# Attention and a feed-forward layer in one kernel: a rebuilt prologue (full-partition weight loads, two load queues, first token tile in two column parts, first output tile K-outer, one batch's loads moved later)

## The chip, the cores and the metric

One core of one Trainium2 chip. The metric is the device time of one execution in microseconds (us), median of several executions; lower is better. In the profiles PE is the matmul engine and PEld its weight loads, DVE is VectorE, ACT ScalarE, POOL GpSimd; SP, the sync engine, only issues transfers (DMA). PSUM is the memory that matmuls write to.

## The reference, cut to what matters

```python
# q, k, v: (8, 8, 576, 64) f32; w_in: (512, 2048); w_out: (2048, 512)
k_p = k.reshape(B, H, 72, 8, D).mean(axis=3)      # 8 keys are averaged into one
v_p = v.reshape(B, H, 72, 8, D).mean(axis=3)
attn = softmax(q @ k_p.T / sqrt(D)) @ v_p         # per batch and head
x = attn.transpose(0, 2, 1, 3).reshape(4608, 512)
h = x @ w_in
out = (h * sigmoid(h)) @ w_out                    # (4608, 512) f32
```

## The kernel before: the parts that matter

The 4608 tokens are cut into 9 tiles of 512; a batch is 576 tokens, so tile t needs the attention of batches up to t. Attention of batch 0 is a prologue. From then on tile t's matmuls carry batch t+1's attention as "fillers", each attached to a step number (0 to 63) of the tile's up-projection (`up`) or down-projection (`down`). Nothing reorders them: an engine's stream is the order of this program.

```python
def load_q(b):                       # f32, two loads of 64 partitions each
    q_raw = big.tile([128, H // 2, QI * D], FP32, tag="q_raw", name="q_raw")   # 2 buffers
    for g in range(2):
        nc.sync.dma_start(out=q_raw[64 * g : 64 * (g + 1), :, :], in_=...)
def load_kv(b):                      # batches 2 to 7: 72 partitions, 1 buffer each
    for name, src in (("k", k), ("v", v)):
        raw = big.tile([SP, H, POOL * D], FP32, tag=f"{name}_raw", bufs=1, name="raw")
        nc.sync.dma_start(out=raw, in_=...)
# (cut) load_kv_flat: batches 0 and 1, k on partitions 0-63 and v on 64-127

def up(t, fillers):                  # (cut) 16 groups of 4 matmuls hp_ps, then Silu -> h_T
def down(t, h_T, fillers):
    for m in range(4):               # one block of 128 tokens after the other
        for g in range(KG):          # 16 matmuls o_ps, K inner
            ...
        nc.vector.tensor_copy(out=o_sb, in_=o_ps)
        # (cut) two stores of 64 partitions on nc.sync

load_q(0); load_kv_flat(0, 3); load_q(1)
# (cut) w_in: 16 loads of 32 partitions on gpsimd; w_out: 4 loads
load_kv_flat(1, 1)
# (cut) attention of batch 0; softmax's division is Ln and Exp on ACT
for t in range(NT):
    a = t + 1
    if a + 1 < B:
        f_up.append((0, lambda: load_q(a + 1)))      # batch t+2, a whole tile ahead
    f_up.append((0, lambda: cast_q(a)))              # GpSimd, f32 -> bf16
    ...
    if a + 1 < B:
        f_up.append((51, lambda: load_kv(a + 1)))
    for n in range(4):                               # PE transposes of the cast q
        f_up.append((20 + 8 * n, lambda n=n: q_transpose(a, n // 2, n % 2)))
```

So in tile 0 the kernel issues batch 2's q, k and v, which tile 1 needs. They are called **batch 2's loads** below.

The softmax here doesn't subtract the row's maximum and nothing guards it: scores larger than these inputs give would overflow.

## Time and profile before

| | before |
|---|---|
| median | 350.74 us (3 runs, 350.31 to 351.3) |
| span of the profiled run | 350.2 us |
| PE busy | 308.6 us, 88% |
| mean granted PE clock | 0.981 |
| up of tile 0 / down of tile 0 / tile 1 / tile 2 start (first matmul in the timeline) | 37.19 / 58.51 / 86.57 / 120.48 us |

The page's rows of 40 slices (each 8.8 us; a digit is tenths):

```profile
PE   0336878499999999999999999999999999999994
PEclk9999989679999999999999999999999999999999
DMA  7999999612866296628653964496420021022022
```

PE is full from the ninth slice on. Ahead of it lie slices full of transfers, and a dip of PE in the eighth, where it waits for `w_out`. Two groups of the page, with busy us and mean ns | idle time before them and what ended it:

```profile
L319 PE MATMUL o_ps<-w_out_sb,h_T 128*128 128x512 bf16 x576 | 142.9, 385 | 6.1 <-DMA w_out_sb<-in_moe_w_out_dram 6.1
L121 PE MATMUL qT_ps<-ident,q_bf 128*128 128x128 bf16 x144 | 14.1, 233 | 12.8 <-POOL q_bf L109 12.7
```

Of the 12.7 us, 10.3 are one wait in the prologue and 2.42 one in tile 0's up; tile 1 has none.

### The profile page before, as it was taken

What the parts mean: (1) busy time and instruction counts of PE and PEld (TensorE: products, weight loads), DVE (VectorE), ACT (ScalarE), POOL (GpSimd) and SP (SyncE); (2) the same over time, 40 slices, a digit from 0 to 9 for tenths busy, and PEclk for the clock granted to TensorE, in tenths of its full rate; (3) what the DMA queues carried; (4) which work ended last, traced back from release to release, by engine and by line L of the source; (5) the groups of instructions that cost most, each with busy time, mean ns of one, the idle gap of its engine ahead of it and who ended that gap; (6) DMA issues with size and microseconds to landing.
All of it is one profiled execution on the core that took longest, in us unless ns stands there. A gap on an engine that the chain in (4) does not pass through costs nothing.

```text
span 350.2 us, 4636 instructions
## 1 busy us (share of the span) xinstructions
PE 308.6 (88%) x1858; PEld 146.0 (42%) x1858; DVE 137.3 (39%) x204; ACT 177.3 (51%) x299; POOL 50.3 (14%) x61
## 2 busy tenths in 40 slices
PE   0336878499999999999999999999999999999994
PEld 0212334144544454445444544454445444444441
DVE  0641651033653456365546553754376231020011
ACT  1026628045675566555755665566566656604600
POOL 2731232000060006000500240033000000000000
PEclk9999989679999999999999999999999999999999
DMA  7999999612866296628653964496420021022022
GB/s 170 223 249 238 238 239 216 121 32 62 176 142 153 59 204 135 154 61 194 138 137 72 204 143 110 93 198 140 96 60 0 21 63 40 0 60 63 0 55 65
DMA packets 21221, 42.24 MB, mean 121 GB/s; under 512 B 2000, under 2 KB 4048, under 8 KB 21072
## 3 DMA queue, kind: packets, MB, share of 16 engines
q1 hardware_dynamic: 17808, 37.76, 47.2%
q0 software_dynamic: 3392, 4.20, 6.8%
q8 instruction: 14, 0.23, 0.3%
q14 instruction: 7, 0.06, 0.1%
HBM read 36.70 MB, written 9.44 MB: 132 GB/s over the span
## 4 chain that ended last, share of the span: by engine, by line
PE 74%; DMA 17%; ACT 4%; POOL 1%; issue 1%; SPq 0%; DVE 0%; POOLq 0%
PE o_ps L319 33%; PE hp_ps L299 32%; DMA w_in_sb<-in_moe_w_in_dram 8%; DMA w_out_sb<-in_moe_w_out_dram 7%; PE sc_ps L235 4%; ACT L277 2%; DMA q_raw<-in_q_dram 2%; PE nu_ps L260 2%; PE den_ps L252 2%; PE qT_ps L121 2%; ACT es L242 1%; ACT h_T L306 1%; POOL q_bf L109 1%; POOL w_out_sb L361 0%; PE kT_ps L165 0%
## 5 line engine op out<-in xcount | busy, mean ns | idle before, releaser
L319 PE MATMUL o_ps<-w_out_sb,h_T 128*128 128x512 bf16 x576 | 142.9, 385 | 6.1 <-DMA w_out_sb<-in_moe_w_out_dram 6.1
L299 PE MATMUL hp_ps<-xT,w_in_sb 128*128 128x512 bf16 x576 | 134.5, 385 | 0.0
L306 ACT ACTIVATE h_T<-hp_ps 128x512 bf16<-128x512 f32 x144 | 85.8, 597 | 70.5 <-PE hp_ps L299 70.4
L319 PEld LDWEIGHTS <-h_T 128*128 128x128 bf16 x576 | 56.2, 99 | 67.4 <-issue 15.8
L299 PEld LDWEIGHTS <-w_in_sb 128*128 128x128 bf16 x576 | 55.4, 99 | 61.6 <-issue 3.9
L272 DVE TENSOR_TENSOR xT<-nu_ps,rec 128x288 bf16<-128x288 f32 x64 | 26.3, 453 | 98.8 <-ACT rec L270 87.5
L109 POOL CAST q_bf<-q_raw 128x576 bf16<-128x576 f32 x32 | 37.0, 1196 | 167.0 <-PE qT_ps L121 118.6
L242 ACT ACTIVATE es<-sc_ps 72x576 bf16<-72x576 f32 x64 | 41.4, 647 | 28.4 <-PE sc_ps L235 28.2
L326 DVE COPY o_sb<-o_ps 128x512 f32<-128x512 f32 x36 | 24.8, 690 | 62.4 <-PE o_ps L319 62.4
L145 DVE TENSOR_TENSOR raw<-raw 72x2048 f32<-72x2048 f32 (+1 forms) x24 | 44.8, 1868 | 0.4
L235 PE MATMUL sc_ps<-qT,kz 128*72 128x288 bf16 x128 | 28.5, 307 | 7.7 <-ACT es L242 7.7
L268 ACT ACTIVATE lnd<-den_ps 128x288 f32<-128x288 f32 x32 | 13.1, 410 | 31.8 <-PE den_ps L252 31.8
L127 DVE COPY qT<-qT_ps 128x640 bf16<-128x640 bf16 (+1 forms) x32 | 14.5, 458 | 35.1 <-PE qT_ps L121 35.1
L121 PE MATMUL qT_ps<-ident,q_bf 128*128 128x128 bf16 x144 | 14.1, 233 | 12.8 <-POOL q_bf L109 12.7
L235 PEld LDWEIGHTS <-kz 128*72 128x72 bf16 x128 | 15.4, 122 | 21.5 <-issue 12.3
L121 PEld LDWEIGHTS <-q_bf 128*128 128x128 bf16 x144 | 11.2, 105 | 20.0 <-POOL q_bf L109 13.6
L260 PE MATMUL nu_ps<-es,vp 72*32 72x288 bf16 x256 | 14.8, 311 | 0.5 <-ACT lnd L268 0.5
L270 ACT ACTIVATE rec<-lnd 128x288 f32<-128x288 f32 x32 | 14.2, 445 | 1.0
L219 ACT COPY vT<-kvT_ps 64x160 bf16<-64x160 bf16 (+1 forms) x8 | 2.2, 274 | 21.5 <-DVE kz L216 21.3
L280 ACT ACT_TABLE_LOAD x9 | 11.5, 1283 | 0.2
L277 ACT ACT_TABLE_LOAD x8 | 10.3, 1283 | 0.9 <-PEq L420 0.7
L351 POOL DMA_DIRECT2D w_in_sb<-in_moe_w_in_dram x16 | 8.6, 544 | 13.8 <-DMA w_in_sb<-in_moe_w_in_dram 13.8
(26 smaller groups left out, 65.5 us busy)
## 6 DMA issues: line engine op xcount, KB each, us to landing
q_raw<-in_q_dram SPq DMA_DIRECT2D x16, 576.0 KB, 7.4
out_dram<-o_sb SPq DMA_DIRECT2D x72, 128.0 KB, 2.3
raw<-in_k_dram SPq DMA_DIRECT2D x6, 1152.0 KB
raw<-in_v_dram SPq DMA_DIRECT2D x6, 1152.0 KB
w_in_sb<-in_moe_w_in_dram POOLq DMA_DIRECT2D x16, 128.0 KB, 16.7
w_out_sb<-in_moe_w_out_dram POOLq DMA_DIRECT2D x4, 512.0 KB, 22.9
kv_raw<-in_k_dram SPq DMA_DIRECT2D x3, 384.0 KB, 10.6
kv_raw<-in_v_dram SPq DMA_DIRECT2D x3, 384.0 KB, 11.7
```

The lines of the kernel that those rows point to most:

```text
L109: nc.gpsimd.tensor_copy(out=q_bf[:, a, :, s, :], in_=st["q_raw"][:, 2 * a + s, :].rearrange("q (i d) -> q i d", d=D),)
L121: nc.tensor.transpose(qT_ps[:, i, :], st["q_bf"][:, a, i0 + i, :, :].rearrange("q s d -> q (s d)"), ident,)
L145: nc.vector.tensor_add(out=raw[:, :, :w], in0=raw[:, :, :w], in1=raw[:, :, w : 2 * w])
L235: nc.tensor.matmul(sc_ps[:, s, :HS], lhsT=kz[b % 2][:, 2 * p + s, :], rhs=st["qT"][:, p, cols], start=True, stop=True,)
L242: nc.scalar.activation(es, sc_ps[:, :, :HS], func=AF.Exp, scale=score_scale)
L260: nc.tensor.matmul(nu_ps[32 * hh : 32 * (hh + 1), :HS], lhsT=st["vp"][:, 4 * g + hh, 32 * c : 32 * (c + 1)], rhs=es[hh // 2][:, hh % 2, :] ...
L272: nc.vector.tensor_mul(out=xT[:, 2 * g + c, cols], in0=nu[c][:, :HS], in1=rec)
L277: nc.scalar.preload_act_table_set("natural_log_exp_and_others")
L299: nc.tensor.matmul(hp_ps, lhsT=w_in_sb[:, kk, g * 128 : (g + 1) * 128], rhs=xT[:, kk, t * NTT : (t + 1) * NTT], start=(kk == 0), stop=(kk ...
L306: nc.scalar.activation(h, hp_ps, func=AF.Silu)
L319: nc.tensor.matmul(o_ps, lhsT=h_T[g][:, m * 128 : (m + 1) * 128], rhs=w_out_sb[:, g, :], start=(g == 0), stop=(g == KG - 1),)
L326: nc.vector.tensor_copy(out=o_sb, in_=o_ps)
```

## The change

It seems meant to shorten the 86 us before tile 1. Weights and q are loaded over all 128 partitions; first loads go out on two queues, k and v ahead of q; the prologue's pipeline has more PSUM buffers, warm-up matmuls and three reciprocals on VectorE; tile 0's up works on the first 288 tokens (batch 0's first half) and then on the other 224; tile 0's down takes three output blocks at once, K-outer (each part of `w_out` is used for all three blocks before the next part is touched), so that it can begin while `w_out` is arriving; the last output block is stored in two column halves. And batch 2's loads move out of the weights' way, to step 50 of tile 0's down. Core of the diff (cuts marked with `...`):

```diff
 def load_q(b, engines=None):
-    for g in range(2):
-        nc.sync.dma_start(out=q_raw[64 * g : 64 * (g + 1), :, :], ...)
+    for e, eng in enumerate(engines):                 # all 128 partitions
+        eng.dma_start(out=q_raw[:, e * n : (e + 1) * n, :], in_=src[:, ...])
 ...
 def load_w_in(...):
-    for hh in (0, 2, 1, 3):
-        for c32 in range(2):
-            nc.gpsimd.dma_start(out=w_in_sb[32 * hh : 32 * (hh + 1), c32::2, cs], ...)
+    for g in range(2):
+        nc.gpsimd.dma_start(out=w_in_sb[:, 2 * g : 2 * g + 2, c0:c1], ...)
 ...
-load_q(0)
-load_kv_flat(0, 3)
-load_q(1)
+load_kv_flat(0, PARTS, [nc.sync, nc.scalar])
+load_q(0, [nc.sync, nc.scalar])
 ...
+nc.gpsimd.tensor_copy(out=gate, in_=batches[0]["kv_raw"][...])   # weights wait for k/v0
 ...
 def values(b, g, f, on_dve=False):
+    if on_dve:
+        nc.vector.reciprocal(rec, den_ps[:, :HS])
+    else:                                             # Ln and Exp on ACT, as before
 ...
-            if a + 1 < B:
+            if a + 1 < B and t:
                 f_up.append((0, lambda: load_q(a + 1)))
 ...
             if a + 1 < B:
-                f_up.append((51, lambda: load_kv(a + 1)))
+                if t:
+                    f_up.append((51, lambda: load_kv(a + 1)))
+                else:
+                    f_down.append((50, lambda: load_kv(a + 1)))
+                    f_down.append((50, lambda: load_q(a + 1)))
 ...
-        h_T = up(t, f_up)
-        down(t, h_T, f_down)
+        h_T = up(t, f_up, (HS, NTT - HS) if t == 0 else (NTT,))
+        down(t, h_T, f_down,
+             [(0, 1, 2), (3,)] if t == 0 else [(m,) for m in range(NTT // 128)],
+             last=t == NT - 1)
```

## The prediction

> **What bounds the kernel now.** I read the page's slices first, then the chain of waits in order of time, then busy time by stage. Nine tiles of 512 tokens each run an up stage (64 matmuls `hp_ps`) and a down stage (64 matmuls `o_ps`), and tile t carries batch t+1's attention between its matmuls. Chain, tile 0 (start us, us, what):
>
> ```profile
> 1.57 7.26 DMA q_raw<-in_q_dram
> ...
> 12.08 9.61 DMA w_in_sb<-in_moe_w_in_dram
> ...
> 21.97 18.17 DMA w_in_sb<-in_moe_w_in_dram
> ...
> 43.73 25.22 DMA w_out_sb<-in_moe_w_out_dram
> ...
> 86.73 4.53 PE hp_ps L299 x21
> ```
>
> Up to 68.95 us the chain is nearly all transfers, from there it is PE. The stages (busy us of each engine, clock, DMA share, GB/s), cut where up of tile 0, its down, and tiles 1 and 2 begin:
>
> ```profile
> 0.00:37.19 37.19, 12.90 (x95) 6.36 (x95) 11.29 (x27) 11.28 (x23) 12.88 (x29) 1.00 1.00 222
> 37.19:58.51 21.32, 18.90 (x100) 8.92 (x97) 11.01 (x14) 11.14 (x21) 8.00 (x12) 0.92 1.07 233
> 58.51:86.73 28.22, 22.14 (x130) 9.55 (x129) 5.29 (x11) 11.78 (x20) 0.00 (x0) 0.82 0.39 86
> 86.73:120.64 33.91, 33.24 (x216) 16.04 (x214) 17.18 (x24) 20.45 (x34) 5.43 (x4) 1.00 0.63 136
> 120.64:154.55 33.91, 33.24 (x216) 16.05 (x214) 17.45 (x24) 20.45 (x34) 6.01 (x4) 1.00 0.61 136
> ```
>
> From 86.73 PE is 98% busy and a tile takes 33.91 us, six times, then two tiles of 27.6 without attention, then 4.7 us of last copy and store. The change hardly touches that. To win are 86.73 - 33.91 = 52.8 us of prologue and stalls in tile 0. There the DMA share is about 1.0 until 58 us. For the rates I cut windows where one kind of transfer runs alone:
>
> ```profile
> 2.00:10.00 8.00, 0.00 (x0) 0.00 (x0) 0.00 (x0) 0.02 (x1) 1.44 (x3) 1.00 1.01 219
> ...
> 62.00:66.00 4.00, 0.23 (x2) 0.04 (x1) 0.00 (x0) 0.65 (x1) 0.00 (x0) 0.77 0.88 185
> 98.00:102.00 4.00, 4.00 (x21) 1.81 (x19) 3.93 (x4) 2.67 (x5) 3.37 (x2) 1.00 0.81 174
> ```
>
> Row one: q and k/v loads of 64 partitions, 219 GB/s at a full share. Row two: `w_out`, 128 partitions. The page counts written bytes and the load casts f32 to bf16, so 185 GB/s is some 370 read. Row three: k of 72 partitions, 174 GB/s, share 0.81. Last, the weight loads' waits on GpSimd (issue view): the ninth `w_in` load waits for the first to land.
>
> ```profile
> 20.49 0.54 POOL L351 DMA_DIRECT2D w_in_sb<-in_moe_w_in_dram  x1 [4.71 <-DMA w_in_sb<-in_moe_w_in_dram]
> ```
>
> **What the Trainium skill says.** (1) "SBUF — State Buffer", Door 1: The DMA port swizzle: a transfer within partitions 0 to 63 reaches 8 of 16 ports, at 1 MiB 196 against 328 GB/s for 128 partitions. The trace agrees: 219 against some 370. So 128-partition loads of weights and q are a real gain. (2) "DMA: Bandwidth & Descriptors", Issuing engines are not separate DMA queues: a second issuing queue saves issue time only. The before kernel has one hardware queue, so no trace shows it. I credit the second queue with little. (3) Same page, Why a DMA increments its semaphore by 16: the engines used are the largest number up to 16 that divides the outer sizes; 72 partitions give 12. Share 0.81 and 174 GB/s agree (12/16 is 0.75). (4) "TensorE: Matmul & The Clock Gate", Part 1: an idle PE falls to half clock and needs some 3.4 us of work to come back. The trace shows a clock of 0.50 from 66 to 72 us after PE's idle stretch.
>
> **The change part by part.** *Bytes.* Before, ahead of the last `w_out` byte were queued q0, k/v0, q1, k/v1, q2, k/v2 (10.6 MB) and 8.4 MB of weights: 19.0 MB read in 67 us, 284 GB/s. After, q2 and k/v2 are issued late in tile 0's down: 15.5 MB remain. k/v0 goes first and alone (the weights are gated on it): 2.36 MB at 219 is 10.8 us, landed near 12.7. The other 13.1 MB at 325 GB/s (what 44 to 55 us of the before trace read, weights counted in f32) take 40 us: `w_out` complete near 51 to 53 us instead of 68.95.
>
> *Prologue.* k/v0 landed 12.7, last pooling part 2.2 us (its four DVE rows at 14 to 20 us), q0 near 17 and cast by 18.5, k copies and q transposes to 20. Scores ran at one pair per 1.4 us, PE and ACT alternating on one buffer; with two buffers ACT's 0.65 us paces them. Eight pairs and four visits then take some 7.5 us instead of 13. Up starts near 27.5 instead of 37.2. It first needs 512 columns of `w_in`.
>
> *Up of tile 0.* The second half of `w_in` is the last load issued of six; sharing with k/v1 and q1 it should land near 39 (SW moved 122 to 172 GB/s read under competition before). Eight column groups of the first part remain: 32 x 0.122 = 3.9 us. The second part, 64 x 0.096 = 6.1 us plus 31 transposes and waits, 2.6 us. Down starts at 39 + 3.9 + 8.7 = 51.6 (before 58.5).
>
> *Down of tile 0.* 33.91 - 13.8 = 20.1 us. K-outer needs the `w_out` parts one after the other over 48 steps, so the last one at 52 us costs nothing; the 11.5 us stalls of before go. It fills all three `mm` banks, so the fourth block waits one DVE copy: + 1.0. Tile 1 starts at 51.6 + 20.1 + 1.0 = 72.7: **14.0 us earlier**.
>
> *Tile 1, the price.* q2 and k/v2 stand in the sync queue behind six stores of the first three output blocks (the listing of the changed queue shows: six stores, k, v, q, two stores). Those blocks now end together at step 48 of 64. Copies of 0.69 us and six issues of 0.56 us put the k issue 4.7 us after step 48, that is about when tile 1 starts. k and v, 2.36 MB at 174 GB/s, take 13.6 us; q2 follows in the same rings, some 3 us, 1.3 for completion, 1.3 for two casts: ready some 19 us into tile 1. PE's first `qT_ps` transpose of tile 1 stands after matmul 20, at 4.4 us. Stall: 19 - 4.4 = **some 15 us**, plus 1.7 for the clock. Before, q2 had landed long ahead.
>
> *Tail.* The last block in two column halves with its copy and stores on two engines: 0.3 us of copy and 0.6 of serial issue, **- 1.0**. The rest (stride-2 `vp` weights, a split last add in the k/v pooling) is off PE's path or tiny.
>
> Sum: 350.7 - 14.0 + 15 + 1.7 - 1.0 = 352.4.
>
> **Rivals.** *A: transfers faster than that.* With 128-partition rows everywhere but k/v and two hardware rings, 13.1 MB could go at 370: 35 us. Then `w_in` lands near 34, down starts near 45 and tile 1 near 66; the stall stays: 345. For it: row two, and the 276 to 290 GB/s written in 24 to 28 us when mixed transfers ran. Against: k/v1 is still 64 partitions wide. K-outer itself is a hint that its writer saw down waiting for `w_out`, that is, early down starts. *B: no stall in tile 1* (k, v and q overlap well, or the stores issue sooner): 336. For it: q3 alone landed in some 8.5 us. Against: three loads of 3.5 MB through rings that move 174 to 219 GB/s can't take under 16 us. *C: q1 or `w_in` late.* If hardware loads crowd the gated weights, `w_in` lands at 45: 358. For it: `w_out` got only about 0.5 MB written in its first 15 us before.
>
> **Range and chances.** The main sum gives 352, A 345, B 336, C 358. Weighted, with A nearly as likely as the main line and C less, 348. Range 337 to 358. Faster needs under 343.7: A with a shorter stall, or B: 0.32. Slower needs over 357.9: C with the full stall: 0.10.
>
> **What would show it.** Down of tile 0 starting at 45 to 54 us and tile 1 at 66 to 75. In tile 1 a PE gap of 10 to 18 us ended by POOL `q_bf` (or DMA `q_raw`), absent before, and a clock of 0.5 behind it: if there is none, the tile 1 step is wrong. `w_out` waits of PE below 2 us (6.1 before). 33.91 us per tile from tile 2 on; if it moves by 0.3, the strided weights matter. A first PE block past 31 us would say that the prologue is not ACT-paced; loads at 219 GB/s throughout would say that the port argument fails.

## More of the kernel before

When batch 2's loads go out is seen in the sync engine's timeline (start us, us, engine, line, operation):

```profile
22.70 1.28 SPq L98 DMA_DIRECT2D q_raw<-in_q_dram  x2
24.03 0.61 SPq L137 DMA_DIRECT2D raw<-in_k_dram  x1
24.68 13.39 SPq L137 DMA_DIRECT2D raw<-in_v_dram  x1
```

At 23 to 25 us (the last issue is held up until 38): long before tile 1, but among the weights.

## The result, and the profile after

The changed kernel took **359.33 us** (median of 4, 358.39 to 359.99) against 351.0 (350.31 to 351.3) of the kernel before in the same rounds: ratio 1.0238, 95% interval 1.021 to 1.0267. Ratios here are the mean time of one kernel's runs over that of the other's of the same rounds, so not quite the ratio of the medians quoted. The change made the kernel slower, and the time lies outside the predicted range. All outputs are right.

The same rows of the page (8.9 us each slice):

```profile
PE   4375698990299999999999999999999999999994
PEclk9565899996589999999999999999999999999999
DMA  7999980079853456536472746283620022022022
```

Three things are new. PE reaches its full digits in the sixth slice, earlier than before. The DMA row has a hole, `00`, in slices 7 and 8. And then PE has a hole of its own, slices 10 and 11 (`02`), with the clock down in 10 to 12. (It is also down in slices 2 to 5, in the prologue.) The chain of waits of the first 140 us names the pieces (start us, us, what):

```profile
19.51 22.46 DMA w_in_sb<-in_moe_w_in_dram
...
42.02 7.53 PE hp_ps L325 x51
...
76.20 18.17 DMA q_raw<-in_q_dram
94.52 1.29 POOL q_bf L126 x2
95.86 0.72 PE qT_ps L135 x5
...
127.84 4.53 PE hp_ps L325 x21
```

Tile 2 starts at 127.84 us on this chain, at 120.64 in the prediction's chain of the kernel before: 7.20 later. From there to the end both take 229.56 us (357.4 - 127.84 and 350.2 - 120.64). The whole loss stands before tile 2. Busy time by stage (busy us of PE, PEld, DVE, ACT, POOL with instruction counts, clock, DMA share, GB/s), cut where up and down of tile 0, tile 1 and tile 2 begin; the last row is the hole in the DMA row:

```profile
0.00:32.70 32.70, 16.04 (x107) 8.16 (x108) 18.12 (x33) 10.29 (x18) 11.01 (x23) 0.69 0.98 221
32.70:56.08 23.38, 19.66 (x160) 15.40 (x159) 8.71 (x20) 12.64 (x36) 2.51 (x4) 0.86 0.91 175
56.08:75.30 19.22, 18.61 (x131) 8.68 (x130) 5.18 (x11) 11.65 (x20) 0.00 (x0) 1.00 0.14 33
75.30:127.84 52.54, 35.97 (x216) 17.09 (x215) 18.19 (x26) 20.45 (x34) 8.24 (x8) 0.84 0.65 159
127.84:161.75 33.91, 33.24 (x216) 16.05 (x214) 18.01 (x26) 20.45 (x34) 5.74 (x4) 1.00 0.54 136
51.00:71.00 20.00, 18.98 (x155) 11.18 (x154) 5.17 (x14) 12.52 (x29) 0.00 (x0) 1.00 0.01 3
```

Row 3: tile 0's down now runs without a stall (before: 28.22 us with 22.14 of PE). Row 4: tile 1 is the loss, 52.5 us for the same 216 PE instructions that take 33.9 in row 5. Row 6: from 51 to 71 us the transfers stand still at 3 GB/s. The loads that tile 1 will wait for could have run in just that time. They had not been issued; the sync engine's timeline:

```profile
71.19 3.71 SPq L342 DMA_DIRECT2D out_dram<-o_sb  x6
74.95 0.60 SPq L151 DMA_DIRECT2D raw<-in_k_dram  x1
75.59 0.50 SPq L151 DMA_DIRECT2D raw<-in_v_dram  x1
76.20 0.41 SPq L111 DMA_DIRECT2D q_raw<-in_q_dram  x1
```

First tile 0's six stores, all at the end because K-outer finishes three blocks together, then k, v and q. Tile 1's first matmul is at 75.26 in the timeline. The three loads, 3 x 1152 KB = 3.54 MB, take until q lands at 94.4: 18.2 us after its own issue and 19.4 after k's, 182 GB/s over all three. The same two groups of the page as before tell the same story:

```profile
L357 PE MATMUL o_ps<-w_out_sb,h_T 128*128 128x512 bf16 (+1 forms) x592 | 140.1, 374 | 0.6 <-DVE o_sb L369 0.5
...
L135 PE MATMUL qT_ps<-ident,q_bf 128*128 128x128 bf16 x144 | 14.3, 236 | 17.0 <-POOL q_bf L126 17.0
```

The waits for `w_out` (6.1 us before) are gone, and the q transposes wait 17.0 us, 15.90 of it at once, for GpSimd's cast, which itself waits for the transfer. One wait was traded for a longer one.

Two smaller lines. In the prologue a reciprocal on VectorE takes 1.95 us, three times; the first of them in the timeline:

```profile
23.10 1.95 DVE L287 RECIPROCAL rec<-den_ps 128x288 f32<-128x288 f32 x1
```

And the tail, in the timeline of the last 20 us:

```profile
351.47 1.91 PE L357 MATMUL o_ps<-w_out_sb,h_T 128*128 128x256 bf16 x16 [0.52 <-DVE o_sb L369]
...
353.42 0.37 ACT L366 COPY o_sb<-o_ps 64x256 f32<-64x256 f32 x1 [13.87 <-DMA out_dram<-o_sb]
...
353.81 0.43 DVE L367 COPY o_sb<-o_ps 64x256 f32<-64x256 f32 x1 [2.40 <-ACT o_sb L366]
```

The two column halves do not overlap: PE's second half waits 0.52 us for the copy of the first. ACT's copy begins when that half ends, at 353.38 (the profile names the first half's store, which lands at 353.41), and VectorE's copy waits for ACT's. The end of the last PE work moves out by 0.7 us and what follows it gets 0.7 shorter.

### The profile page after: what moved, and what is told of

Read it like the earlier page. It is cut to its first block, busy times and chain, and to the rows that moved or that the text cites. A ratio compares the mean times of both kernels' runs of the same rounds, so it can differ in the third digit from the quotient of the medians.

```text
span 357.4 us, 4845 instructions
## 1 busy us (share of the span) xinstructions
PE 311.9 (87%) x1950; PEld 156.0 (44%) x1950; DVE 145.2 (41%) x229; ACT 178.0 (50%) x311; POOL 44.7 (13%) x51
## 4 chain that ended last, share of the span: by engine, by line
PE 74%; DMA 16%; ACT 6%; POOL 1%; SPq 1%; DVE 1%; issue 0%; POOLq 0%
PE hp_ps L325 33%; PE o_ps L357 31%; DMA q_raw<-in_q_dram 9%; DMA w_in_sb<-in_moe_w_in_dram 6%; PE sc_ps L252 4%; ACT L298 3%; PE qT_ps L135 2%; PE den_ps L269 2%; PE nu_ps L278 2%; ACT h_T L331 1%; ACT es L259 1%; POOL q_bf L126 1%; POOL w_in_sb L399 1%; DMA out_dram<-o_sb 1%; SPq L200 0%
## 5 line engine op out<-in xcount | busy, mean ns | idle before, releaser
L325 PE MATMUL hp_ps<-xT,w_in_sb 128*128 128x512 bf16 (+2 forms) x640 | 137.7, 368 | 6.4 <-DMA w_in_sb<-in_moe_w_in_dram 3.2
L357 PE MATMUL o_ps<-w_out_sb,h_T 128*128 128x512 bf16 (+1 forms) x592 | 140.1, 374 | 0.6 <-DVE o_sb L369 0.5
L331 ACT ACTIVATE h_T<-hp_ps 128x512 bf16<-128x512 f32 (+2 forms) x160 | 88.4, 555 | 93.7 <-PE hp_ps L325 93.0
L325 PEld LDWEIGHTS <-w_in_sb 128*128 128x128 bf16 x640 | 62.6, 101 | 64.5 <-issue 4.6
L126 POOL CAST q_bf<-q_raw 128x576 bf16<-128x576 f32 x30 | 35.0, 1207 | 190.2 <-PE qT_ps L135 120.6
L369 DVE COPY o_sb<-o_ps 128x512 f32<-128x512 f32 (+1 forms) x36 | 24.4, 682 | 59.8 <-PE o_ps L357 59.7
L252 PE MATMUL sc_ps<-qT,kz 128*72 128x288 bf16 x128 | 26.8, 298 | 5.2 <-ACT es L259 4.5
L291 ACT ACTIVATE rec<-lnd 128x288 f32<-128x288 f32 x29 | 12.8, 443 | 0.9
L159 DVE TENSOR_TENSOR kv_raw<-kv_raw 128x768 f32<-128x768 f32 (+1 forms) x12 | 9.0, 754 | 9.6 <-DMA kv_raw<-in_v_dram 9.3
L269 PE MATMUL den_ps<-es,ones 72*32 72x288 bf16 x128 | 10.2, 304 | 0.0
```

What stands on the lines that cost most here:

```text
L126: nc.gpsimd.tensor_copy(out=dst, in_=src)
L159: nc.vector.tensor_add(out=raw[:, :, :w], in0=raw[:, :, :w], in1=raw[:, :, w : 2 * w])
L252: nc.tensor.matmul(sc_ps[:, u, :HS], lhsT=kz[b % 2][:, p, u, :], rhs=st["qT"][:, p, cols], start=True, stop=True,)
L325: nc.tensor.matmul(hp_ps[:, :n], lhsT=w_in_sb[:, kk, g * 128 : (g + 1) * 128], rhs=xT[:, kk, t * NTT + n0 : t * NTT + n0 + n], start=(kk = ...
L331: nc.scalar.activation(h_T[g][:, n0 : n0 + n], hp_ps[:, :n], func=AF.Silu)
L357: nc.tensor.matmul(ps[:, cs], lhsT=h_T[g][:, m * 128 : (m + 1) * 128], rhs=w_out_sb[:, g, cs], start=(g == 0), stop=(g == KG - 1),)
```

## The experiments

**Theory A**: the move of batch 2's loads to the end of tile 0's down makes the loss. The rest of the rebuild is worth little or nothing in itself; the earlier start of tile 1 comes from the same move, which leaves the weights alone on the DMA engines. **Rival B**: the rebuild itself gains about 14 us, and the price is in its new parts (K-outer bunching the stores, the split tile 0, the reciprocals, a lower clock), so that the loads are only one of several costs. The runs fall in three calls, each with the kernel before beside them: 351.13 us for the runs 1 to 4, 350.55 in both other calls.

### 1. The changed kernel with the loads ahead of tile 0's stores, held until `w_out` has landed (e1_gated)

```diff
+            if after_w_out and name == "k":     # one element: k's load now waits for w_out
+                nc.gpsimd.tensor_copy(out=raw[:, 0, :1], in_=w_out_sb[:SP, KG - 1, :1])
 ...
-                    f_down.append((50, lambda: load_kv(a + 1)))
-                    f_down.append((50, lambda: load_q(a + 1)))
+                    f_down.append((0, lambda: load_kv(a + 1, after_w_out=True)))
+                    f_down.append((0, lambda: load_q(a + 1)))
```

> The changed kernel with one move: batch 2's k, v and q loads stand ahead of the output stores in the sync queue, held back only until the last w_out part has landed (51 us in the changed kernel's trace). Theory A (the 15.9 us gap of PE in tile 1 is the late issue of these three loads at 74.95 us): gap and half clock go, tile 2 starts near 109 instead of 127.8, time 359.3 - 18.5 = about 341. Rival B (the tile 1 delay comes from the rate of the loads or from contention, not from when they are issued): some gap stays, time above 350.

Measured: **341.31 us** (339.05 to 342.66), ratio 0.9729 (0.9661 to 0.9797). The sync engine's timeline:

```profile
52.78 0.38 SPq L153 DMA_DIRECT2D raw<-in_k_dram  x1
53.20 0.44 SPq L153 DMA_DIRECT2D raw<-in_v_dram  x1
53.75 0.40 SPq L111 DMA_DIRECT2D q_raw<-in_q_dram  x1
```

Issued 22 us sooner, in the hole. Tile 1 starts at 75.6 us, as in the changed kernel (75.3), and takes 33.91 us instead of 52.4. The earlier issue alone makes 18 us: theory A's size, and more than the loss.

### 2. The same move without the hold (e1_early)

```diff
-                    f_down.append((50, lambda: load_kv(a + 1)))
-                    f_down.append((50, lambda: load_q(a + 1)))
+                    f_down.append((0, lambda: load_kv(a + 1)))
+                    f_down.append((0, lambda: load_q(a + 1)))
```

> The same move without the hold: the sync engine is free from 20.4 us, so the three loads are issued there and then and share the engines with w_in and w_out, as in the kernel before. Theory A: no gap in tile 1, but w_out lands near 62 instead of 51 us and w_in a few us later; as K-outer uses w_out late, tile 1 starts near 77.5, time about 343. Rival (the hold matters, because w_out then stalls down): PE waits for w_out over 4 us and time is over 347.

Measured: **341.69 us** (340.14 to 343.09), ratio 0.9746 (0.9687 to 0.9805). The loads now go out in the midst of the weights, about where the kernel before has them:

```profile
21.00 0.63 SPq L151 DMA_DIRECT2D raw<-in_k_dram  x1
22.18 0.32 SPq L151 DMA_DIRECT2D raw<-in_v_dram  x1
24.87 18.33 SPq L111 DMA_DIRECT2D q_raw<-in_q_dram  x1
```

Tile 1 starts at 74.95 and takes 33.91. So in the changed kernel the early place is as good as the hold: PE does not wait for `w_out`. Yet `w_out` is late here too; the view of its tile:

```profile
L413 POOL DMA_DIRECT2D w_out_sb<-in_moe_w_out_dram x4: 745/758/770, 20.1 to 24.5; - x4
DMA to landing us min/median/max: 29.6/37.3/41.3
```

The last part, issued at 24.5, takes 41.3 us and lands at 65.8 (52.5 with the hold, 68.95 in the kernel before). In the K-outer order PE comes to that part with its 37th matmul of the first three blocks, at 66.98 us; in block order it would be the 13th, which ran at 59.64. From these three times the K-outer order hides some 6 us here, as the expectation had it (an estimate; no run has early loads with block order, so this is argued and not shown).

The run also refutes the second half of theory A: with these loads about where the kernel before has them (only their order differs), the rebuild alone brings the early start of tile 1, and 9.4 us (351.13 to 341.69). Most of it is in tile 0's down, which takes 19.2 us instead of the 28.1 of the kernel before.

### 3. The changed kernel with tile 0's down in block order, loads still late (e2_mouter)

```diff
-            [(0, 1, 2), (3,)] if t == 0 else [(m,) for m in range(NTT // 128)],
+            [(m,) for m in range(NTT // 128)],
```

> The changed kernel with tile 0's down stage back in block order, loads still at step 50. Two stores instead of six then stand between step 48 and the k issue. Theory A: the issue is some 2.5 us earlier, the gap in tile 1 shrinks from 15.9 to 13 to 14 us, and no w_out wait appears, since w_out landed at 51 us before down began at 56: time about 356.5. Rival (K-outer is what saves the w_out waits): PE waits for w_out in tile 0's down and time is over 360.

Measured: **357.8 us** (356.14 to 358.59), ratio 1.0201 (1.0147 to 1.0254), an interval that overlaps the changed kernel's. k is issued at 71.63 instead of 74.95, but tile 1 starts at 73.60 and its gap is still 15.21 us (13 to 14 had been expected). The bunched stores are not the main cause; from q's issue to its landing it takes 19.1 us here, 18.2 in the changed kernel. PE has no wait for `w_out` here either: with the loads late, the K-outer order has nothing to hide.

### 4. The kernel before with only batch 2's loads made late (e3_before_late)

```diff
-            if a + 1 < B:
+            if a + 1 < B and t:
                 f_up.append((0, lambda: load_q(a + 1)))
 ...
-                f_up.append((51, lambda: load_kv(a + 1)))
+                if t:
+                    f_up.append((51, lambda: load_kv(a + 1)))
+                else:
+                    f_down.append((50, lambda: load_kv(a + 1)))
+                    f_down.append((50, lambda: load_q(a + 1)))
```

> The kernel before with one part of the change alone: batch 2's loads moved behind the stores of tile 0's down stage (step 50). Theory A: PE's 6.1 us of w_out waits in tile 0 go, as 3.5 MB less stand ahead, tile 1 starts near 76, and a gap of 13 to 17 us ended by the q cast appears in tile 1: time 353 to 358. Rival B (the gap needs the K-outer order or the new pools): no gap, time 340 to 345.

Measured: **363.52 us** (362.37 to 364.17), ratio 1.0367 (1.0318 to 1.0415); slower than expected. PE's timeline in tile 1:

```profile
100.61 0.72 PE L121 MATMUL qT_ps<-ident,q_bf 128*128 128x128 bf16 x5 [21.88 <-POOL q_bf L109]
```

This is the strongest run for the theory. Tile 1 starts at 74.04 us: the move alone, with nothing of the rebuild, brings as early a start as the whole change (75.3), and the same kind of loss behind it. (Run 2 has the same start from the rebuild without the move: each is enough alone, and the two do not add up.) The gap is 21.88 instead of the 15.9 of the changed kernel. Here q comes as two loads of 64 partitions and lands 25.1 us after issue, against 19.1 in run 3 with the same block order. That the shape of q's load makes the 6 us is likely but not isolated; it would be the one place where a part of the rebuild shows a gain, in a wait that the change itself made.

### 5. The kernel before with only batch 2's loads held for `w_out` (e5_before_gated)

The schedule lines of run 4, with step 0 for step 50, and the hold of run 1:

```diff
+                    f_down.append((0, lambda: load_kv(a + 1, after_w_out=True)))
+                    f_down.append((0, lambda: load_q(a + 1)))
```

> The kernel before, nothing rebuilt, with batch 2's loads taken out of the prologue and issued when the last w_out part has landed (a one-element copy holds them). Theory A (the rebuild's whole gain at the start of tile 1 is the 3.5 MB that no longer stand ahead of w_out): tile 1 starts near 74, as in the run with the late loads, no gap follows, time 351 - 12.7 = about 338.5, no worse than the rebuilt kernel with the same hold (341.3). Rival (the other parts of the rebuild earn several us): time above 344.

Measured: **341.08 us** (340.6 to 341.57), ratio 0.9739 (0.9704 to 0.9774): some 2.5 above what was expected, and equal to run 1 (0.9729). Tile 1 starts at 73.67 us, two us sooner than with the rebuild, and has a short wait:

```profile
79.99 0.45 PE L121 MATMUL qT_ps<-ident,q_bf 128*128 128x128 bf16 x5 [1.62 <-POOL q_bf L109]
```

With the loads held, the kernel before and the rebuilt one are equal within the spread: what the rebuild gains in run 2 and what the hold gains here are the same time, won in two ways. Rival B's 14 us, on top of well-placed loads, are not there.

### 6. The kernel before with only the shape of the `w_in` loads changed (e4_before_fullw)

```diff
-        for hh in (0, 2, 1, 3):
-            for c32 in range(2):
-                nc.gpsimd.dma_start(out=w_in_sb[32 * hh : 32 * (hh + 1), c32::2, cs], ...)
+        for g in range(2):
+            nc.gpsimd.dma_start(out=w_in_sb[:, 2 * g : 2 * g + 2, cs], ...)
```

(with the source view and the rows that `vp` feeds permuted to match)

> The kernel before with only the w_in loads rebuilt: 4 loads over 128 partitions in place of 16 over 32 (w_in rows and the value columns permuted to match). Theory A (tile 0 is bound by the bytes ahead of the last w_out part, not by the shape of the weight loads): w_in lands some us earlier, w_out moves by under 4 us, time 347 to 351. Rival (the partition count doubles the rate of the weights): w_out lands 10 us earlier, time about 340.

Measured: **350.48 us** (349.57 to 350.62), ratio 1.0002 (0.9958 to 1.0045): nothing. PE still waits for `w_out` behind the other bytes, 7.9 us in all:

```profile
59.33 0.59 PE L319 MATMUL o_ps<-w_out_sb,h_T 128*128 128x512 bf16 x1 [3.23 <-DMA w_out_sb<-in_moe_w_out_dram]
65.28 1.86 PE L319 MATMUL o_ps<-w_out_sb,h_T 128*128 128x512 bf16 x4 [3.60 <-DMA w_out_sb<-in_moe_w_out_dram]
68.24 1.01 PE L319 MATMUL o_ps<-w_out_sb,h_T 128*128 128x512 bf16 x2 [1.10 <-DMA w_out_sb<-in_moe_w_out_dram]
```

### 7. Run 1 with batch 1's k, v and q held until `w_in` has landed (e7_gated_hold)

```diff
         raw = big.tile([128, KI, POOL * D], FP32, tag="kv_raw", bufs=1, name="kv_raw")
+        if b == 1:
+            nc.gpsimd.tensor_copy(out=raw[:, 0, :1], in_=w_in_sb[:, KF - 1, d_ff - 1 :])
```

> The changed kernel with batch 2's loads held for w_out (341.3 us) and also batch 1's k, v and q held until w_in has landed. Theory: with k/v1 and q1 out of the way w_in lands near 27 instead of 42 us, so up of tile 0 no longer waits for it (3.4 us) and runs on from 32.5; q1 then lands near 45 and bounds its second part: down starts near 52 instead of 56, time about 337. Rival (q1 or k/v1 becomes the wait): time 341 or more, with PE waiting for the q cast in tile 0.

A miss: **348.29 us** (347.28 to 350.54), ratio 0.9954 (0.9902 to 1.0006). `w_in` lands by 29.5 us and PE no longer waits for it, but batch 1's q comes at 52.35, and the same kind of gap appears one tile earlier:

```profile
53.68 0.71 PE L135 MATMUL qT_ps<-ident,q_bf 128*128 128x128 bf16 x5 [8.49 <-POOL q_bf L126]
```

Holding a load back is good only as long as its consumer is further off than the transfer takes.

### 8. Run 1 without the two halves of the last block (e6_gated_plain_tail)

```diff
-            last=t == NT - 1,
+            last=False,
```

> The changed kernel with batch 2's loads held for w_out, and the last output block plain again (no column halves). In the changed kernel's trace the halves gained nothing: from the start of tile 2 to the end it takes 229.56 us, as before. Theory: within 0.3 us of 341.3. Rival (the halves save the 1.0 us of the prediction): 342.3.

Measured: **341.5 us** (340.94 to 342.02), ratio 0.9751 (0.9716 to 0.9786). Against run 1's 0.9729 that is no measurable gain of the halves, as the timeline above says.

### 9 to 12. Run 1 with single parts of the rebuild taken back

Run 9 (e8_gated_act) puts the three reciprocals back on ACT:

```diff
-        values(0, 0, 0, on_dve=True)
+        values(0, 0, 0)
 ...
-            values(0, g, 1, on_dve=True)
+            values(0, g, 1)
```

> The gated version with all reciprocals of the prologue back on ACT (as in the kernel before). Theory: the up-projection starts sooner (29 to 30 us instead of 32.7), but the landing of w_in at 42 us bounds it, so the time is 341 us within 0.5. Rival: the prologue's chain counts in full: 338 to 339 us.

Measured: **340.7 us** (340.25 to 342.55), ratio 0.9735 (0.9673 to 0.9797). The prologue does get 3 us shorter (up starts at 29.23 us instead of 32.51), and nothing comes of it, because up then stands here, in PE's timeline:

```profile
41.61 7.45 PE L327 MATMUL hp_ps<-xT,w_in_sb 128*128 128x288 bf16 x51 [2.40 <-DMA w_in_sb<-in_moe_w_in_dram]
```

Run 10 (e9_gated_unsplit) does tile 0's up in one part:

```diff
-        n0 = KG * KF if t == 0 else 0
+        n0 = 0
 ...
-        h_T = up(t, f_up, (HS, NTT - HS) if t == 0 else (NTT,))
+        h_T = up(t, f_up, (NTT,))
```

> The gated version with tile 0's up-projection in one part instead of two column parts. Theory (estimate): w_in lands at 42.4 us whatever the PE does, and after it the split version still has about 10.0 us of up-projection matmuls to run (3.9 of part 0 and 6.1 of part 1), the unsplit one 32 matmuls of 0.216 = 6.9 us; so down starts about 3 us sooner and the time is about 338.5 us. Rival: the second part of the tokens (q1, landed 39.8 in the gated version) now has to be there before the first matmul, and the clock is lower after the longer wait, so nothing is gained: 341 to 343 us.

Measured: **338.89 us** (337.78 to 339.8), ratio 0.9672 (0.9612 to 0.9732), the fastest of all. PE's timeline of up:

```profile
34.11 7.28 PE L327 MATMUL hp_ps<-xT,w_in_sb 128*128 128x512 bf16 x21 [2.73 <-DVE xT L295]
42.10 0.45 PE L135 MATMUL qT_ps<-ident,q_bf 128*128 128x128 bf16 x5 [0.70 <-POOL q_bf L126]
```

While the transfers run, 21 matmuls of all 512 columns are done; the split version spends that time on 34 of 288 columns, which is less work (34 x 288 = 9792 columns against 21 x 512 = 10752). Down starts at 53.12 instead of 56.45. The theory's size was right; its reason only in part. The wait that ends last is now that for batch 1's q, not for `w_in`. And the 960 columns are only some 0.4 us (an estimate, at 4.53 us for 21 matmuls of 512), while 1.7 of the 3.3 us are the clock: the 51 matmuls behind run 1's wait took 7.53 us in its trace and 5.86 in run 11's, where down starts at 54.82. Tile 1 gives back 0.75 (34.66 instead of 33.91 us). The intervals of runs 1 and 10 overlap, so that the unsplit form is faster at all is likely, not shown.

Run 11 (e10_gated_onequeue) issues all first loads on the sync engine's queue:

```diff
-        load_kv_flat(0, PARTS, [nc.sync, nc.scalar])
-        load_q(0, [nc.sync, nc.scalar])
+        load_kv_flat(0, PARTS, [nc.sync, nc.sync])
+        load_q(0, [nc.sync, nc.sync])
```

> The gated version with all first loads issued on the one sync queue, none on ACT's. Theory: the same within 1 us (340 to 342), because the 16 engines are shared and w_in's landing is set by the bytes ahead of it. Rival: the first batch's k and v land later and everything after them shifts: 343 us or more.

Measured: **341.31 us** (339.54 to 341.81), ratio 0.9747 (0.9679 to 0.9815): the same. The second queue earns nothing, as "DMA: Bandwidth & Descriptors", Issuing engines are not separate DMA queues (the prediction's second citation), leads one to expect and as no trace had shown until now.

Run 12 (e12_gated_plain) takes all of that back together: the edits of runs 3, 8, 9 and 10 on run 1.

> The gated version with the other parts of the rebuild taken back together: tile 0 unsplit, reciprocals on ACT, first output tile in block order, plain last tile; what remains is full-partition weight loads, two queues and the early, held loads of the second batch. Theory: 337 to 338 us, the fastest of all, since none of the removed parts earns anything once the second batch is there in time. Rival: unsplit tile 0 waits for q1 and gives 341 or more.

Measured: **339.84 us** (339.53 to 340.88), ratio 0.9705 (0.9647 to 0.9764). It beats both kernels, but not run 10 (338.89; their runs overlap). The expectation of 337 to 338 failed. Up starts at 28.55 us, down only at 54.57, since PE then waits 5.58 us for batch 1's q.

### The runs in one table

Tile 1's start and length are from the first matmul of each tile in the timeline.

| | batch 2's loads issued, us | tile 1 starts, us | tile 1 takes, us | median, us |
|---|---|---|---|---|
| before | 23-25 | 86.6 | 33.9 | 351.0 |
| before, loads late (run 4) | 72-74 | 74.0 | 58.6 | 363.5 |
| before, loads held (run 5) | 54-56 | 73.7 | 35.7 | 341.1 |
| changed | 75-76 | 75.3 | 52.4 | 359.3 |
| changed, loads early (run 2) | 21-25 | 75.0 | 33.9 | 341.7 |
| changed, loads held (run 1) | 53-54 | 75.6 | 33.9 | 341.3 |
| held, tile 0 unsplit (run 10) | 53-54 | 72.3 | 34.7 | 338.9 |

In the kernel before, these loads can be too early (their bytes delay `w_out`, for which PE waits) and too late. In the changed kernel only "too late" costs, since run 2 is as fast as run 1: its early loads delay `w_out` nearly as much (65.8 against 52.5 us when held; 68.95 against 54.0 in the kernel before), but K-outer asks for the parts later (argued from run 2's trace; not taken apart by a run).

## Why the prediction was wrong

The mechanism was right: k, v and q behind six stores, issued when tile 1 starts, a PE gap in tile 1 ended by POOL `q_bf`, half clock behind it, `w_out` complete near 51 to 53 us (52.1) and its waits gone, 33.91 us a tile from tile 2 on. All of these are in the profile. Two steps failed.

**One is the last, the weighting** (4.4 us): "Weighted, with A nearly as likely as the main line and C less, 348." The prediction's own sum was 352.4, already slower than before, and it was then drawn down to 348 towards two rivals:

- Rival A, "`w_in` lands near 34 ... tile 1 near 66": `w_in` landed at 42.0 and tile 1 began at 75.3. The rate hoped for came neither from shape (run 6: 1.0002) nor from the second queue (run 11).
- Rival B, "no stall in tile 1": its own text says that the three loads "can't take under 16 us". They took 18.2 after q's issue. That argument should have ruled B out, not left it with weight. The high end, 358, was taken from one rival alone and left no room for several terms to miss in the same direction.

**The other is the sum itself** (5.5 us): three of its terms were too good, the start of tile 1 most of all:

| term, as predicted | predicted, us | measured, us | what the runs showed |
|---|---|---|---|
| start of tile 1, "14.0 us earlier" | -14.0 | -11.3 | below |
| stall and clock in tile 1, "some 15 us", plus 1.7 for the clock | +16.7 | +18.5 | gap 15.90; PE busy 35.97 instead of 33.24 behind it, at a lower clock, 2.7 |
| tail in halves | -1.0 | 0 | serial, as the timeline shows; run 8 |
| sum from 350.7 | 352.4 | 357.9 | |

The measured terms make +7.2, and the spans differ by 7.2 (357.4 and 350.2); the medians differ by 8.3, the rest being spread between runs.

The start of tile 1 missed as follows. "Up starts near 27.5", paced by ACT, was 32.70: the prediction overlooked that the diff puts three reciprocals on VectorE, 1.95 us each, one after the other. They are 3.3 of the 5.2 us (run 9 takes them back); the rest was not taken apart. Run 9 also shows that this part of the miss cost nothing. "`w_in` should land near 39" was 42.0 (3 us), and that did count, for up cannot end before it. Behind it, 51 matmuls took 7.53 us at a mean clock of 0.77; in runs 2, 3 and 11 the same 51 took 5.86, so the clock's share is 1.7. "Down starts at 51.6" was therefore 56.08. Down itself took 19.2 us where 20.1 + 1.0 had been allowed, which gives 1.9 back.

**A premise was wrong as well, and it is the more useful one.** The prediction takes the late loads as part of what frees `w_out` (its byte count, 19.0 MB before and 15.5 after) and as the price of that. Run 4 takes only those bytes away, in the kernel before, and has tile 1 at 74.0: the bytes are reason enough. But run 2 puts them back in the changed kernel and has it at 75.0. So in the changed kernel the late loads bought no earlier start; they were price alone. Its other reason, "128-partition loads of weights and q are a real gain", is not borne out for `w_in`: run 6 changes that shape for `w_in` and gets nothing. The reading behind it, "The trace agrees: 219 against some 370", sets bytes written beside bytes read; in bytes written, the `w_out` loads over 128 partitions ran at 185 GB/s (share 0.88), no faster than the 219 of the loads over 64. Held until `w_out` has landed (runs 1 and 5), some 20 us before the late place, the loads keep the early start without the price; in the changed kernel, loads issued earlier still do so too (run 2).

## What to carry to other kernels

When a change moves a transfer, write down three times for it: when its bytes compete with something urgent, when its consumer comes, and how long it takes; then look in the DMA row for an idle stretch between the first two. A load attached to the end of a stage lands a whole transfer time after the next stage began, and queued behind stores it is later still. Before crediting a rebuild of many parts, try the lines of it that move bytes alone on the kernel before, and take them back alone in the changed one. Here the first gave the early start and the loss with nothing rebuilt, and the second gave the early start without the loss.

## What the Trainium skill lacked or had wrong

- "ScalarE: Activation LUTs", What it computes: the page says to use VectorE's reciprocal for `Reciprocal`, but neither it nor a VectorE page gives its duration. Here a 128x288 f32 reciprocal from PSUM took 1.95 us on VectorE, against 0.41 for Ln and 0.44 for Exp on ACT, which do the same division.
- "SBUF — State Buffer", Door 1: The DMA port swizzle, gives rates of one transfer by the partitions that it reaches. With many loads in flight they did not tell what the shape of one was worth: sixteen `w_in` loads of 32 partitions and four of 128 gave the same time (ratio 1.0002), and from 11 to 49 us 238 and 239 GB/s moved in all, at a DMA share of 1.06 in both.
- No page says how the placing of a load (too early among urgent bytes, too late for its consumer) is to be read from a profile. Here it was worth 22 us (363.5 in run 4, 341.1 in run 5), with the same instructions but for a one-element copy.
